# A one-byte constant in DRAM for the accumulating transfers, up to two transfers for a quad, eight term buffers, MLP evictions ahead, and a new order of an attention and token-MLP kernel

## The chip, the core and the metric

The kernel runs on one core of one Trainium2 chip. Its engines work side by side, each with an instruction queue of its own: TensorE (PE, matmuls, with its weight loads as PEld), VectorE (DVE), ScalarE (ACT), GpSimd (POOL), and SyncE (SP), which mostly issues DMAs. 16 DMA engines move data for all of them. They meet by semaphores. Matmul results stand in PSUM, which has eight banks of 512 float32 columns. The metric is device microseconds (us) of the whole program, given as the median of several runs. A profile is one further execution.

## The reference

```python
xn = layernorm(A_x)                                  # 2048 rows of 640
def A(x, wqkv, wo):                                  # attention: 32 heads of 20
    q, k, v = (x @ wqkv) split into heads
    p = softmax(q k^T * 20 ** -0.5)                  # 2048 x 2048 for each head
    return (p v, heads side by side) @ wo
def B(x, w1, b1, w2, b2):                            # MLP across the 2048 rows
    u = gelu(einsum("bsd,sf->bdf", layernorm(x), w1) + b1)      # f = 1536
    return transpose(einsum("bdf,fs->bds", u, w2) + b2)
return A_x + A(xn, wqkv, wo) * silu(B(xn, w1, b1, w2, b2))
```

Most of the work is the exponentials of the scores: 32 heads x 2048 x 2048.

## The kernel before

**Tiling.** Heads are taken in eight groups of four. A pass is one group and 512 query columns, 33 passes in all (the last 512 columns are done in two halves). A unit is one head, 128 keys and 512 queries: a score matmul (L1343) fills one PSUM bank with it. There are 2048 units. Four units of one key chunk, one for each head of the group, are a quad.

**Two ways to an exponential.** Most units go to ACT: one activation (L1373, `emit_exp`) takes two or three banks at once and writes `pt_sb`, and a matmul with V (L1459, `emit_pv`) sums it up in bank 6. The other units go to DVE by whole quads. There L1384 (`emit_op1`) turns a bank of scores into 16-bit whole numbers, which read as bf16 are a power of two made of straight pieces; four such units make one term tile `dt_sb[b]` of 4 x 512. Three more copies of the tile, raised by 32, 64 and 96, are made, and each of the four is multiplied with its own scaled V (`vs_sb`) at L1459: a quad thus costs sixteen V matmuls where four units by ACT cost four, and the mean of the four shifted lines is close to the exponential. A copy is one DVE addition (L1437, `emit_top`) into another tile. For some quads the last copy, +96, is not made by DVE: once PE has read the first tile, `emit_x` (L1408) lets POOL issue a DMA that adds a constant tile `kc_sb` (in SBUF, 16-bit, all 96) onto the first tile in place. `x_ok` says for which quads: XQ limits how far the transfers may lag, XLEFT how near the pass's end may be.

**The rest.** At the start DVE takes the statistics of the 16 row blocks (L586 to L604), POOL the powers of the variances (L600), and PE and ACT or DVE bring the transposed rows, Q, K and V into place. The MLP's matmuls (L705) and the QK and V projections of later heads run between the score matmuls in bank 7, and DVE takes them out of it (L880, L1171, L1174) or, in the start alone, ACT may (L1170, L1173). At the end the output projection (L1022) and the stores stand behind the last pass.

**What sets the order.** Nothing is scheduled on the chip: `Prog` plays the program through when it is built, with a cost for each operation, and the order that comes out is written into the engines' queues. At each step the engine that can start first takes, among its candidates, the one with the lowest priority number (`eng_cands`, `pe_cands`). A transfer is charged 950 ns of POOL, 2,900 ns of the DMA engines, and lands 5,600 ns after that (XISSUE, XMOVE, XTAIL at L48); its readers are put behind that. PLAN is a table of digits: for every 16 units claimed, `tune` sets the planner's options in OPTS by one string of it. A transfer on POOL waits for PE's reads of the tile, and the next transfer waits in POOL's queue behind it. DMAs of SP go around eight lanes, and each waits for the one before it on its lane.

Of the kernel before, what the change touches and what calls it, by code (L numbers as in the profile page):

```python
# [283 lines left out]
class _Kern:  # L284
# [9 lines left out]
    JB = 7  # L294
    RC = (1, 4, 7, 10, 13)
# [42 lines left out]
    NTILE, NLIVE, EARLY = 7, 4, True  # L338
    DLAG = 99.0
    OTA, OTD = 25.0, 0.16  # L340
    XLEFT, XQ = 20, 4000.0
    QC = ((0.5, 3.0), (3.2, 6.4), (9.0, 13.5), (14.0, 18.0), (19.0, 22.0))
# [19 lines left out]
        ("JOBF", (4, 0, 8)),  # L362
    )
    PLAN = (
        "000000000000000", "000000000000000", "000000000000000", "000000000000000", "100000000000000", "100000000000000",
        "000030000000000", "000000000000000", "000000000000000", "000030000000000", "000000000000001", "000000000000000",
        "012000000000000", "020000300000000", "002020000000000", "020000000000000", "210041000000002", "210041000000002",
        "210041000000002", "000000000000000", "000004000000000", "002020000000000", "201000000000001", "000201000000000",
        "012000000000000", "000001000000000", "000020000000000", "000030000000000", "000030000000000", "200201000000000",
        "000030000000000", "000040200000000", "000001000000000", "000000000000000", "000000000000000", "210041000000002",  # L370
        "000001000000000", "020000000000000", "010031000000002", "010000000000000", "012000000000000", "000000000010000",
        "012000000000000", "000000000000000", "120000000010000", "100000000000000", "000000000000200", "012000000000000",
        "000000000000000", "000000000000000", "000030000000000", "200000000000000", "000000000000000", "000030000000000",
        "000000000000000", "000030000000000", "000000000000000", "020000000000000", "000000000000000", "010040000000000",
        "010040000000000", "100004000000000", "000000000000000", "000104300000000", "000000000000000", "000030000000000",
        "210041000000002", "012000000000000", "000000000000000", "000001000000000", "010040000000000", "100000000000000",
        "000001000000000", "000001000000000", "000000000000000", "000050000000000", "000000000000000", "000030000000000",
        "000000000000000", "100000000000000", "000000000000000", "020000000000000", "000030000000000", "000000000000000",
        "000000000000000", "000030000000000", "000000000000000", "200041000000000", "010040000000000", "400100000000000",
        "000040000010000", "000000000000000", "000004000001000", "020000000000000", "000000000000000", "400000000000100",  # L380
        "200041000000000", "000000000000000", "000000000000000", "000004000000000", "000000300001001", "012020000000000",
        "012000000000000", "012000000000000", "000030000000000", "000000000000000", "100000000000000", "000000000000000",
        "002040000000000", "000030000000000", "000000000000000", "000030000000000", "000001000000000", "000030000000000",
        "000000000000000", "000000000000000", "010040000000000", "012000000000000", "000040000000000", "000040000000000",
        "012000000000000", "000000000000000", "000000000000000", "000040000000000", "000000000000000", "000001000000000",
        "000000000000000", "001201000000001",
# [19 lines left out]
    def build(self):  # L406
# [4 lines left out]
        with es:  # L411
# [20 lines left out]
            sb("kc_sb", [P, 4, 512], u16)  # L432
# [15 lines left out]
            t["oT_dram"] = nc.dram_tensor("oT_scratch_dram", [8 * P, S], bf)  # L448
            t["ok_dram"] = nc.dram_tensor("ok_scratch_dram", [S, 512], bf)
# [17 lines left out]
    def schedule(self):  # L467
# [719 lines left out]
        kc_sb = t["kc_sb"]  # L1187
# [216 lines left out]
        def emit_x(d):  # L1404
            b0 = d["tl"][0]
            dst = dt_sb[:, b0, :, :]
            sl_ = [S_(f"dt{b0}_{g}") for g in range(4)]
            t = pr.xdma(lambda e: e.dma_start(dst, kc_sb[:, :, :], accum_op=ALU.add), [S_("kc")] + sl_, sl_,  # L1408
                        f"dX{d['q']}_{d['c']}")
            d["tl"][3] = b0  # L1410
            d["fin"][3] = t.fin
            stats["x"] = stats.get("x", 0) + 1

        def emit_top():
# [75 lines left out]
        def emit_pv(items, quads):  # L1490
# [6 lines left out]
            for d, n_ in quads:  # L1497
                for k in range(d["pk"], d["pk"] + n_):
                    for g in range(4):
                        seq.append(("d", d, k, g))  # L1500
                    if k > (1 if self.MERGE else 0) or d["tl"][3] is not None:
                        freed.append(d["tl"][k])
# [44 lines left out]
            for d in xs:  # L1547
                emit_x(d)
# [759 lines left out]
```

## Time and profile before

| | |
|---|---|
| median of 3 runs | 745.08 us (745.07 to 745.76) |
| span of the profiled execution | 743.6 us |
| median less that span | 1.5 us |
| ACT, DVE, PE busy | 721.9, 706.5, 706.2 us |
| activations of two and of three banks | 514 and 168 |
| units by DVE | 516 (129 quads) |
| copies by DVE and by transfers | 323 and 64 |

The three runs are of the unprofiled program; the span is that of the profiled execution, from its first to its last instruction. Sums below are made against the span, and what lies around it is taken as unchanged. In the profile an engine's busy time is the union of its instructions; the mean time of one instruction is longer than the step from one to the next where two overlap. The row "A <- B: us, times, longest" of the view of waits reads: A's engine stood idle until B released it.

### The profile page before, as it was taken

Reading aid. Unit: us, or ns where it says so; the run is one execution under the profiler, and the core shown is the slowest. Engines: PE = TensorE matmul, PEld = TensorE weight load, DVE = VectorE, ACT = ScalarE, POOL = GpSimd, SP = SyncE. Lnnn points to the kernel's source line nnn. Section 1 sums busy time; section 2 is a strip of 40 time slices with the busy share of each in tenths; the row PEclk is TensorE's granted clock in tenths of the full one; section 3 lists DMA queues with packets and bytes.
Section 4 is the critical chain, followed back from the end, with each engine's and each line's share of the span. In section 5 each row is a group of like instructions: output and inputs, shape, how many; then the busy total and the mean of one; then the engine's idle time right before and its main releaser. Section 6 shows DMA issues by size and latency. Waiting matters only on the chain.

```text
span 743.6 us, 23596 instructions
## 1 busy us (share of the span) xinstructions
PE 706.2 (95%) x10472; PEld 238.1 (32%) x10486; DVE 706.5 (95%) x1295; ACT 721.9 (97%) x708; POOL 74.9 (10%) x88
## 2 busy tenths in 40 slices
PE   8899999999999989999999999999999999999997
PEld 7332222222332322323232232323333233233333
DVE  8998999999999999999999899999999999999998
ACT  5999999999999999999999999999999999999995
POOL 5300100000010000000000000011000100110000
PEclk9999999999999999999999999999999999999999
DMA  8767544432364444446234394647447993364212
GB/s 238 140 149 84 114 95 93 77 67 47 83 146 77 87 81 85 112 80 133 42 69 87 71 175 75 133 75 159 101 92 126 144 161 61 63 186 101 70 49 72
DMA packets 128955, 76.23 MB, mean 103 GB/s; under 512 B 80196, under 2 KB 119492, under 8 KB 128804
## 3 DMA queue, kind: packets, MB, share of 16 engines
q1 hardware_dynamic: 119636, 41.15, 25.3%
q0 software_dynamic: 9216, 33.56, 25.0%
q8 instruction: 82, 1.34, 0.7%
q14 instruction: 21, 0.17, 0.1%
HBM read 26.37 MB, written 10.22 MB: 49 GB/s over the span
## 4 chain that ended last, share of the span: by engine, by line
ACT 71%; PE 21%; DVE 4%; DMA 3%; issue 1%; SPq 0%; POOL 0%
ACT pt_sb L1373 69%; PE ps_all L1459 7%; PE ps_all L1343 6%; PE ps_all L705 6%; DMA dt_sb<-kc_sb 1%; DVE dt_sb L1384 1%; ACT zt_sb L906 1%; DMA bload_sb<-in_B_b_dram 1%; DVE dt_sb L1437 1%; ACT zt_sb L901 1%; PE ps_all L1022 1%; PE ps_all L690 0%; DMA regA<-in_A_x_dram 0%; SPq L1626 0%; DVE qk_sb L1174 0%
## 5 line engine op out<-in xcount | busy, mean ns | idle before, releaser
L1373 ACT ACTIVATE pt_sb<-ps_all 128x1024 bf16<-128x1024 f32 (+1 forms) x682 | 703.5, 1227 | 4.9 <-PE ps_all L1343 3.5
L1384 DVE TENSOR_SCALAR dt_sb<-ps_all 128x512 uint16<-128x512 f32 x516 | 343.0, 683 | 20.9 <-PE ps_all L1343 14.5
L1343 PE MATMUL ps_all<-qk_sb 32*128 32x512 bf16 (+1 forms) x2128 | 268.7, 376 | 22.7 <-ACT pt_sb L1373 20.1
L1437 DVE TENSOR_SCALAR dt_sb<-dt_sb 128x2048 uint16<-128x2048 uint16 x323 | 212.0, 688 | 1.6
L1343 PEld LDWEIGHTS ps_all<-qk_sb 32*128 32x128 bf16 x2128 | 67.9, 91 | 277.9 <-ACT pt_sb L1373 221.3
L1459 PE MATMUL ps_all<-dt_sb,vs_sb 128*21 128x512 bf16 (+1 forms) x1596 | 137.7, 376 | 1.3 <-DMA dt_sb<-kc_sb 0.9
L1459 PE MATMUL ps_all<-pt_sb,v_sb 128*21 128x512 bf16 (+1 forms) x1596 | 124.9, 374 | 1.3 <-DVE v_sb L1171 0.7
L1408 POOL DMA_DIRECT2D dt_sb<-kc_sb x64 | 58.4, 912 | 608.0 <-PE ps_all L1459 338.2
L705 PE MATMUL ps_all<-regC,regA 128*32 128x128 bf16 (+1 forms) x1444 | 66.5, 296 | 1.4 <-issue 1.3
L705 PE MATMUL ps_all<-regB,regA 128*32 128x128 bf16 (+1 forms) x1476 | 67.7, 297 | 0.0
L1459 PEld LDWEIGHTS ps_all<-dt_sb,vs_sb 128*21 128x21 bf16 x1596 | 35.9, 90 | 53.8 <-issue 31.2
L1459 PE MATMUL ps_all<-dt_sb,v_sb 128*21 128x512 bf16 (+1 forms) x532 | 50.7, 376 | 0.0
L705 PE MATMUL ps_all<-xnT_sb,wqk_sb 128*32 128x512 bf16 x640 | 47.7, 382 | 0.2 <-DVE qs_sb L1171 0.2
L1459 PEld LDWEIGHTS ps_all<-pt_sb,v_sb 128*21 128x21 bf16 x1596 | 29.5, 90 | 46.8 <-issue 33.4
L705 PEld LDWEIGHTS ps_all<-regB,regA 128*32 128x32 bf16 x1476 | 27.7, 96 | 24.2 <-issue 12.5
L713 PE MATMUL ps_all<-regC,regA 32*128 32x512 bf16 x92 | 35.4, 384 | 0.0
L705 PEld LDWEIGHTS ps_all<-regC,regA 128*32 128x32 bf16 x1444 | 27.1, 96 | 23.8 <-issue 12.8
L1022 PE MATMUL ps_all<-wv_sb,xnT_sb 128*128 128x128 bf16 (+1 forms) x150 | 25.6, 295 | 1.4 <-issue 1.4
L705 PE MATMUL ps_all<-wv_sb,xnT_sb 128*32 128x480 bf16 x320 | 22.8, 369 | 0.5 <-DVE v_sb L1171 0.5
L713 PE MATMUL ps_all<-regB,regA 32*128 32x512 bf16 x60 | 23.1, 385 | 0.0
L1587 DVE STREAM_TRANSPOSE tr_sb<-ps_all 128x512 f32<-128x512 f32 x31 | 22.0, 709 | 0.5 <-PE ps_all L1459 0.5
L705 PEld LDWEIGHTS ps_all<-xnT_sb,wqk_sb 128*32 128x32 bf16 x640 | 13.6, 95 | 19.2 <-issue 8.8
(88 smaller groups left out, 360.5 us busy)
## 6 DMA issues: line engine op xcount, KB each, us to landing
dt_sb<-kc_sb POOLq DMA_DIRECT2D x64, 512.0 KB, 5.5
regA<-in_B_w_dram SPq DMA_DIRECT2D x6, 1024.0 KB
regA<-in_B_w_dram SPq DMA_DIRECT2D x8, 768.0 KB
qk_sb<-qk_scratch_dram SPq DMA_DIRECT2D x56, 80.0 KB
qk_scratch_dram<-qs_sb SPq DMA_DIRECT2D x32, 128.0 KB
regA<-in_A_x_dram SPq DMA_DIRECT2D x6, 640.0 KB
ok_scratch_dram<-on_sb SPq DMA_DIRECT2D x96, 20.0 KB
out_dram<-regC SPq DMA_DIRECT2D x3, 640.0 KB
```

Of the source, the lines that this page charges most:

```text
L705: fns.append(lambda e, c=c, e_=e_: e.matmul(oc(c, e_), lhsT[:, c:e_], rhs, start=start, stop=stop, tile_position=(0, c)))
L713: row = lambda g: (lambda e: e.matmul(oc(0, 128), lhsT[32 * g:32 * g + 32, :], rhs[32 * g:32 * g + 32, :], start=False, stop=False, tile_p ...
L901: steps.append(("act", lambda e: e.activation(tt_, tt_, AF.Tanh, scale=1.5957691216), [stt], [stt], f"th{j}", ac(n)))
L906: steps.append(("act", lambda e: e.activation(tt_, z, AF.Tanh), sz, [stt], f"th2_{j}", ac(n)))
L1022: steps.append(("pe", lambda e, c=c: e.matmul(ap, oT_sb[:, c, b * 128:(b + 1) * 128], wo_ap[:, c, c0:c0 + n], start=(opens and c == 0), st ...
L1343: t = pr.pe(lambda e, outp=outp, lhsT=lhsT, rhs=rhs, g=g: e.matmul(outp, lhsT, rhs, start=True, stop=True, tile_position=(32 * g, 0)), rea ...
L1373: tk = pr.act(lambda e: e.activation(outp, inp, AF.Exp, scale=math.log(2.0) / 128.0), reads=[bank_slot[b] for b in banks[:n]], writes=[S_( ...
L1384: tk = pr.dve(lambda e: e.tensor_scalar(w, src, WOFF, 0.0, ALU.add, ALU.max), reads=[bank_slot[bk]], writes=[S_(f"dt{d['tl'][0]}_{g}")], n ...
L1408: t = pr.xdma(lambda e: e.dma_start(dst, kc_sb[:, :, :], accum_op=ALU.add), [S_("kc")] + sl_, sl_, f"dX{d['q']}_{d['c']}")
L1437: tk = pr.dve(lambda e: e.tensor_scalar(dst, src, dk, None, ALU.add), reads=[S_(f"dt{b}_{g}") for b in inb for g in range(4)], writes=[S_( ...
L1459: pr.pe(lambda e: e.matmul(outp, lhsT, rhs, start=(k == 0), stop=last, tile_position=(0, 32 * g)), reads=reads, writes=[bank_slot[AB]], na ...
L1587: steps.append(("dve", lambda e: e.transpose(tr_sb[:, :], ps(AB)), [bank_slot[AB]], [S_("tr")], f"epT{q}", 632.0))
```

## The change

Six edits. The constant for the accumulating transfers is no longer a 16-bit tile in SBUF: POOL fills two rows of 64 16-bit words with the bytes 96 and 64 (`kc_sb`, 256 bytes for each partition instead of 4,096), and two DMAs of SP spread them into a DRAM tensor `kc_dram` of bytes; a transfer reads 2,048 bytes for each partition there and widens them to 16 bits while it adds. The 8th term tile takes the place of the old constant (NTILE 7 to 8). A quad may give two copies to transfers: DVE then makes only the +32 copy, and when PE has read the first tile, +64 is added to it in place, and when PE has read the +32 tile, +64 is added to that (96 in all); `x2_ok` decides with XLEFT2 and XQ2. DVE's MLP work that holds a bank gets the priority number EVJ (36 or less, by the plan 19 or 45) where it had 45 (`eng_cands`). Six more options stand in the plan, and its table is another one.

```diff
-    NTILE, NLIVE, EARLY = 7, 4, True
+    NTILE, NLIVE, EARLY = 8, 4, True
+    EVJ = 36.0
+    XLEFT2, XQ2 = 40, 1000.0
...
+        ("EVJ", (36.0, 19.0, 45.0)),
+        ("XLEFT", (20, 14, 28, 99)),
+        ("XLEFT2", (40, 32, 26, 99)),
+        ("XQ2", (1000.0, 3000.0)),
+        ("NLIVE", (4, 5, 6)),
+        ("D_GUARD", (8, 16, 24)),
...
-        "000030000000000", "000000000000000", "000000000000000", "000030000000000", "000000000000001", "000000000000000",
+        "000000000000000000000", "000000000000000000001", "000000000000000003000", "000000000000000000000", "000000000000000000000", "010031000000002000000",
...
-            sb("kc_sb", [P, 4, 512], u16)
+            sb("kc_sb", [P, 2, 64], u16)
+            t["kc_dram"] = nc.dram_tensor("kc_scratch_dram", [2 * P, 2048], dt.uint8)
...
+        def x2_ok(d):
+            if "kc" not in done or pr.xpipe > pr.T["dve"] + self.XQ2:
+                return False
+            return d["q"] > a_cur[0] or a_left(d["q"]) >= self.XLEFT2
+
-        def emit_x(d):
-            b0 = d["tl"][0]
+        def emit_x(d, k0, k1):
+            b0 = d["tl"][k0]
+            i = 0 if k1 - k0 == 3 else 1
             dst = dt_sb[:, b0, :, :]
+            src = kc_dram[i * P:(i + 1) * P, :].rearrange("p (g n) -> p g n", g=4)
             sl_ = [S_(f"dt{b0}_{g}") for g in range(4)]
-            t = pr.xdma(lambda e: e.dma_start(dst, kc_sb[:, :, :], accum_op=ALU.add), [S_("kc")] + sl_, sl_,
-                        f"dX{d['q']}_{d['c']}")
+            t = pr.xdma(lambda e: e.dma_start(dst, src, accum_op=ALU.add), [S_(f"kc{i}")] + sl_, sl_,
+                        f"dX{d['q']}_{d['c']}_{k1}")
...
+        def feed_x(d):
+            if d["x"] == 1 and d["pk"] >= 1 and d["tl"][3] is None:
+                emit_x(d, 0, 3)
+            if d["x"] == 2 and d["pk"] >= 1 and d["tl"][2] is None:
+                emit_x(d, 0, 2)
+            if d["x"] == 2 and d["pk"] >= 2 and d["tl"][3] is None:
+                emit_x(d, 1, 3)
...
-            if k == 2 and not self.MERGE and x_ok(d):
-                d["x"] = True
+            if k == 1 and not self.MERGE and x2_ok(d):
+                d["x"] = 2
                 dtop.pop(0)
-                if d["pk"] >= 1:
-                    emit_x(d)
+                feed_x(d)
+            elif k == 2 and not self.MERGE and x_ok(d):
+                d["x"] = 1
+                dtop.pop(0)
+                feed_x(d)
...
-        add_job("kc", [("pool", lambda e: e.memset(kc_sb[:, :, :], int(self.DK[3])), [], [S_("kc")], "kc", 1800.0), ("tag", "kc")],
-                (), 43.0)
+        kcl = []
+        for i in (0, 1):
+            kcs = bass.AP(kc_sb, 64 * i, [[128, P], [0, 16], [1, 64]]).bitcast(dt.uint8)
+            kcd = kc_dram[i * P:(i + 1) * P, :].rearrange("p (r n) -> p r n", r=16)
+            kcl.append(("pool", lambda e, i=i: e.memset(kc_sb[:, i, :], int(self.DK[3 - i]) * 257), [], [S_(f"kcs{i}")], f"kcs{i}", 150.0))
+            kcl.append(("dma", lambda e, kcd=kcd, kcs=kcs: e.dma_start(kcd, kcs), [S_(f"kcs{i}")], [S_(f"kc{i}")], f"kc{i}", 262144))
+        add_job("kc", kcl + [("tag", "kc")], ("qk0_0_3",), 41.0)
...
-                    c.append((j.prio, pr.ready(eng, s[2], s[3]), lambda j=j: do_step(j, eng)))
+                    p_ = min(j.prio, self.EVJ) if eng == "dve" and j.bk is not None and not ramp[0] else j.prio
+                    c.append((p_, pr.ready(eng, s[2], s[3]), lambda j=j: do_step(j, eng)))
```

In the built program this gives, of activations, 516 of two banks and 164 of three (514 and 168 before), so 1,524 units by ACT where there were 1,532; on DVE 524 units at L1384 (516), 317 copies (323); on POOL 76 transfers (64); on PE 24 more V matmuls that read term tiles and 8 fewer that read `pt_sb`. By the planner's own count 24 quads give two copies to transfers and 28 give one (0 and 64 before).

The first place is ACT's queue in the start of the program, from its first exponential on (`pt_sb`); `qk_sb` and `v_sb` are taken out of PSUM there. Before:

```order
L1373 ACTIVATE pt_sb<-ps_all 128x1536
L1173 ACTIVATE qk_sb<-ps_all 128x256
L1170 ACTIVATE qk_sb<-ps_all 128x256
L1373 ACTIVATE pt_sb<-ps_all 128x1536 x4
L1170 ACTIVATE qk_sb<-ps_all 128x256
L1373 ACTIVATE pt_sb<-ps_all 128x1536
L1170 ACTIVATE qk_sb<-ps_all 128x256
L1373 ACTIVATE pt_sb<-ps_all 128x1536 x11
L1373 ACTIVATE pt_sb<-ps_all 128x1024 x4
```

And with the change:

```order
L1382 ACTIVATE pt_sb<-ps_all 128x1536 x2
L1179 ACTIVATE v_sb<-ps_all 128x2x8x20
L1382 ACTIVATE pt_sb<-ps_all 128x1536 x2
L1179 ACTIVATE qk_sb<-ps_all 128x256
L1382 ACTIVATE pt_sb<-ps_all 128x1536
L1179 ACTIVATE qk_sb<-ps_all 128x256
L1382 ACTIVATE pt_sb<-ps_all 128x1536 x9
L1179 ACTIVATE qk_sb<-ps_all 128x256
L1179 ACTIVATE v_sb<-ps_all 128x8x20
L1382 ACTIVATE pt_sb<-ps_all 128x1536 x2
L1382 ACTIVATE pt_sb<-ps_all 128x1024 x5
```

Three evictions have come over from DVE: one of V (320 columns) into the first run of four exponentials, and one of Q or K (256) and one of V (160) two activations before the end of the run of eleven.

The second place is POOL's queue, from the fill of the ones in `v_sb` on. Before:

```order
L568 MEMSET v_sb 128x512x2
L1643 MEMSET kc_sb 128x2048
L600 TENSOR_TENSOR st_sb<-st_sb,cst_sb 128x2 x6
L622 TENSOR_TENSOR st_sb<-st_sb,cst_sb 128x8
L1835 MEMSET idb_sb 128x128
L1408 DMA dt_sb<-kc_sb 128x2048 x44
L1757 MEMSET wqk_sb 128x640
L1408 DMA dt_sb<-kc_sb 128x2048 x20
```

And with the change:

```order
L577 MEMSET v_sb 128x512x2
L609 TENSOR_TENSOR st_sb<-st_sb,cst_sb 128x2 x6
L631 TENSOR_TENSOR st_sb<-st_sb,cst_sb 128x8
L1868 MEMSET idb_sb 128x128
L1675 MEMSET kc_sb 128x64 x2
L1424 DMA dt_sb<-kc_scratch_dram 128x2048 x52
L1790 MEMSET wqk_sb 128x640
L1424 DMA dt_sb<-kc_scratch_dram 128x2048 x24
```

The fill of the constant no longer stands ahead of the first powers of the variances; two short fills stand behind all of them, and twelve more transfers follow.

The third place is PE's queue where it first waits for transfers (`sem_x0` to `sem_x3` tell of them); `dt_sb,vs_sb` are V matmuls of a copy, `qk_sb` are score matmuls. Before:

```order
L705 MATMUL ps_all<-xnT_sb,wqk_sb 32x512 x19
L1459 MATMUL ps_all<-dt_sb,vs_sb 21x512 [waits sem_x0]
L1459 MATMUL ps_all<-dt_sb,vs_sb 21x512 x3
L1343 MATMUL ps_all<-qk_sb 128x512 [waits sem_act]
L1343 MATMUL ps_all<-qk_sb 128x512 x2
```

And with the change:

```order
L1352 MATMUL ps_all<-qk_sb 128x512 [waits sem_dve]
L1487 MATMUL ps_all<-dt_sb,vs_sb 21x512 [waits sem_x0]
L1487 MATMUL ps_all<-dt_sb,vs_sb 21x512 x3
L1487 MATMUL ps_all<-dt_sb,vs_sb 21x512 [waits sem_x1]
L1487 MATMUL ps_all<-dt_sb,vs_sb 21x512 x3
L1352 MATMUL ps_all<-qk_sb 128x512 [waits sem_act]
```

Where PE waited for one transfer and then went on to scores, it now takes the copies of two transfers in a row.

More of the change, by code (lines that the diff above doesn't have):

```diff
@@ L367 @@
[L367 to L371, printed above, removed]
@@ L1186, in schedule @@
         tfree = list(range(self.NTILE))
-        kc_sb = t["kc_sb"]
+        kc_sb, kc_dram = t["kc_sb"], t["kc_dram"]
         dlive = [0]
@@ L1500, in emit_pv @@
                         seq.append(("d", d, k, g))
[L1501 removed]
+                    if k > (1 if self.MERGE or d["x"] == 2 else 0) or (d["tl"][3] is not None and not d["x"]):
                         freed.append(d["tl"][k])
                 d["pk"] += n_
[L1504 removed]
+                if d["x"]:
                     xs.append(d)
@@ L1903, in pe_cands @@
                 k = 0
-                while k < len(quads) - 1 and quads[k][1]["x"] and quads[k][1]["pk"] == 3:
+                while k < len(quads) - 1 and quads[k][1]["x"] and quads[k][1]["pk"] >= 4 - quads[k][1]["x"]:
                     k += 1
@@ L2045, in dve_load @@
             for d, k in dtop:
-                x += (1730.0 if k == 1 else 1130.0) if self.MERGE else 600.0 * ((3 if x_ok(d) else 4) - k)
+                x += (1730.0 if k == 1 else 1130.0) if self.MERGE else 600.0 * ((2 if k == 1 and x2_ok(d) else 3 if x_ok(d) else 4) - k)
             return x
@@ L2211, in loads @@
                 d += (1730.0 if x["fin"][1] == 0.0 else 1130.0 if x["fin"][3] == 0.0 else 0.0) if self.MERGE else (
-                    597.0 * sum(f == 0.0 for f in x["fin"][1:3 if x["x"] else 4]))
+                    597.0 * sum(f == 0.0 for f in x["fin"][1:4 - (x["x"] or 0)]))
             return a - done_cost["act"], pe - done_cost["pe"], d - done_cost["dve"]
```

45 lines of the change are left out of this document (25 added, 20 removed).

## The prediction

> **What bounds the kernel now.** First the page's busy times, its chain of waits, and the program cut into three stretches (columns: length, then busy time and instructions of PE, weight loads, DVE, ACT, POOL, then clock, DMA share, GB/s).
>
> ```profile
> span 743.6 us, 23596 instructions
> PE 706.2 (95%) x10472; PEld 238.1 (32%) x10486; DVE 706.5 (95%) x1295; ACT 721.9 (97%) x708; POOL 74.9 (10%) x88
> ...
> ACT 71%; PE 21%; DVE 4%; DMA 3%; issue 1%; SPq 0%; POOL 0%
> ```
>
> ```profile
> 0.00:26.00 26.00, 21.69 (x248) 15.96 (x248) 22.63 (x80) 16.65 (x21) 12.80 (x20) 1.00 0.88 201
> 26.00:730.00 704.00, 674.66 (x10085) 216.89 (x10098) 673.37 (x1195) 700.46 (x684) 62.09 (x69) 1.00 0.50 99
> 730.00:744.00 14.00, 9.81 (x140) 5.26 (x140) 10.46 (x23) 4.81 (x5) 0.00 (x0) 1.00 0.27 95
> ```
>
> Between 26 and 730 us ACT is idle 704.0 - 700.5 = 3.5 us, PE 29.3 and DVE 30.6. So ACT sets the length of the middle, and a change there is worth what it takes off ACT as long as PE and DVE keep feeding it. They have 4% to spare each, in pieces; PE's 21% of the chain says that it often releases ACT at the last moment. The start (ACT idle 9.4 us of 26) and the end (9.2 of 14) are set by other things. The clock is 1.00 throughout.
>
> **The exponentials.** The groups by shape price a unit (count, then busy time, mean ns of one, idle before):
>
> ```profile
> L1373 ACT ACTIVATE pt_sb<-ps_all 128x1024 bf16<-128x1024 f32 x514 | 498.0, 1124 | 1.9 <-PE ps_all L1343 1.0 <-PE ps_all L713 0.2
> L1384 DVE TENSOR_SCALAR dt_sb<-ps_all 128x512 uint16<-128x512 f32 x516 | 343.0, 683 | 20.9 <-PE ps_all L1343 14.5 <-PE ps_all L713 4.2
> L1373 ACT ACTIVATE pt_sb<-ps_all 128x1536 bf16<-128x1536 f32 x168 | 250.5, 1543 | 3.0 <-PE ps_all L1343 2.4 <-PE ps_all L1459 0.3
> L1437 DVE TENSOR_SCALAR dt_sb<-dt_sb 128x2048 uint16<-128x2048 uint16 x323 | 212.0, 688 | 1.6
> ```
>
> ```profile
> L1373 ACT ACTIVATE pt_sb<-ps_all 128x1024 bf16<-128x1024 f32 (+1 forms) x682 | 703.5, 1227 | 4.9 <-PE ps_all L1343 3.5
> ```
>
> A third bank adds 1543 - 1124 = 419 ns. The 682 activations hold 514 x 2 + 168 x 3 = 1,532 units, 641.9 us at that price; the other 61.6 us of 703.5 are 90 ns for each activation. The change leaves 516 and 164: eight units and two activations fewer, 3.35 + 0.18 = **-3.5 us**. Bounds: -3.35 (units alone) and -4.5 (8 x 1124 / 2). Two quads more go to DVE instead.
>
> **Evictions moved onto ACT.** Three in the start: 320, 256 and 160 columns.
>
> ```profile
> 12.37 1.44 ACT L1373 ACTIVATE pt_sb<-ps_all 128x1536 bf16<-128x1536 f32 x1
> ...
> 15.29 5.48 ACT L1373 ACTIVATE pt_sb<-ps_all 128x1536 bf16<-128x1536 f32 x4 [0.92 <-PE ps_all L1343]
> 20.63 0.42 ACT L1170 ACTIVATE qk_sb<-ps_all 128x256 bf16<-128x256 f32 x1
> 21.53 1.45 ACT L1373 ACTIVATE pt_sb<-ps_all 128x1536 bf16<-128x1536 f32 x1 [0.48 <-PE ps_all L1343]
> 22.88 0.38 ACT L1170 ACTIVATE qk_sb<-ps_all 128x256 bf16<-128x256 f32 x1
> 23.14 4.14 ACT L1373 ACTIVATE pt_sb<-ps_all 128x1536 bf16<-128x1536 f32 x3
> ```
>
> The one at 22.88 holds the next exponential back 0.26 us for 256 columns; 736 columns make 0.75 us if ACT has no gap for them, and nothing where they fall into gaps like those of 0.92 and 0.48. I take **+0.6**, since two of the three now stand in a run without gaps.
>
> **The fill of the constant leaves the start.** Rows of POOL, DVE and PE in order of time (start, length):
>
> ```profile
> 2.76 2.86 POOL L568 MEMSET v_sb<- 128x1024 bf16 x1
> 5.36 1.96 POOL L1643 MEMSET kc_sb<- 128x2048 uint16 x1
> 7.43 1.59 POOL L600 TENSOR_TENSOR st_sb<-st_sb,cst_sb 128x2 f32<-128x2 f32 x2
> ```
>
> ```profile
> 5.79 1.56 DVE L597 TENSOR_SCALAR st_sb<-st_sb 128x2 f32<-128x2 f32 x1
> 5.84 1.50 DVE L586 BATCH_NORM_STATS2 bst_sb<-regA 128x6 f32<-128x320 bf16 x1
> ...
> 7.65 0.17 DVE L597 TENSOR_SCALAR st_sb<-st_sb 128x2 f32<-128x2 f32 x1
> 8.18 0.80 DVE L604 TENSOR_SCALAR regC<-regA,st_sb 128x640 bf16<-128x640 bf16 x2 [0.36 <-POOL st_sb L600]
> ```
>
> ```profile
> 8.69 0.81 PE L656 MATMUL ps_all<-idb_sb,regC 128*128 128x128 bf16 x10 [1.29 <-DVE regC L604]
> ```
>
> ```profile
> 7.34 0.54 ACT L785 ACTIVATE wp_sb<-wqk_sb 128x400 bf16<-128x400 bf16 x1 [0.70 <-DMA wqk_sb<-in_A_wqkv_dram]
> ```
>
> The first power at 7.43 stands in POOL's queue behind the fill, which ends at 7.32. What it reads, L597, takes 0.17 us the second time but 1.56 the first, ending with the fill too. Without the fill POOL is free at 5.62 and L597 done at about 5.96, so the power, DVE's row scaling, and the transposes for which PE waits 1.29 us come up to 7.43 - 6.05 = 1.4 us sooner. What is late next: the second weight copy ends at 7.88, before the Q and K matmuls would need it; the later row blocks come by DMA, and the first stretch's DMA share of 0.88 leaves those little room. So between 0 and -1.4; I take **-1.0**, nearer the full step because ACT runs almost without a gap from 23 us on and keeps what it has gained by then.
>
> **PE.** 24 more V matmuls on term tiles (32 of two quads, less 8 of eight units). Two pieces of the chain:
>
> ```profile
> 497.52 0.54 PE ps_all L1459 x8
> ...
> 498.38 0.76 PE ps_all L1459 x12
> ```
>
> Four more cost 0.22 us, so 24 cost 1.3 us. They lie in PE's 29 us of idle time, but by its 21% of the chain I charge **+0.3** (bounds 0 and 1.3).
>
> **DVE.** Eight more L1384 at 343.0 / 516 = 0.66 us and six fewer L1437 at 212.0 / 323 = 0.66: +1.3 us, hidden in 30 us of idle time, 0 (+1.3 if that cover is gone).
>
> **The transfers.**
>
> ```profile
> q0 software_dynamic: 9216, 33.56, 25.0%
> ```
>
> ```profile
> L1408 POOL DMA_DIRECT2D dt_sb<-kc_sb x64: 872/872/1510, 51.2 to 700.9; - x64
> ...
>   PEld ps_all L1459: 1.2, 1
>   PE ps_all L1459: 0.9, 1
> ...
> DMA to landing us min/median/max: 4.5/5.5/11.1
> ```
>
> ```profile
> 0.00:10.00 10.00, 7.51 (x70) 6.82 (x70) 6.71 (x22) 3.09 (x5) 8.08 (x14) 1.00 0.79 232
> ```
>
> A transfer takes 0.25 x 743.6 / 64 = 2.9 us of all 16 DMA engines. The plain loads of the first 10 us run at 232 / 0.79 = 294 GB/s, by which 512 KB take 1.8 us. With half the source bytes it should cost 1.8 to 2.9, unless widening bytes is slower; no row shows that. POOL's 12 more issues at 0.87 us fit its 642 us of idle time in the middle. The price is the landing. The planner keeps readers 0.95 + 2.9 + 5.6 = 9.45 us behind the issue, more behind a queue of transfers; the median landing is 5.5, and of 64 only one made PE wait, 1.2 us. So +4 us would be hidden in the median case: I take 0.
>
> The source now lies in DRAM. [...]
>
> **The stores of the constant, EVJ, the new order.** The two DMAs stand on SP behind the small bias loads and ahead of the first Q/K stores, and the first transfers wait for them. SP waits a few rows ahead for work of DVE anyway,
>
> ```profile
> SPq L1601 <- DVE on_sb L1595: 12.8, 1, 12.8
> ```
>
> and DVE makes the copies until then, which the 317 contain. EVJ adds no instruction: an MLP eviction goes ahead of a copy (38), which frees bank 7 earlier and the copy's reader later, both hidden by PE's other candidates. What the new order does to ACT's waits I set to 0, with bounds of 3.5 us either way: it can save no more than the 3.5 us of idle time, and I let it lose as much.
>
> **Sum.** -3.5 + 0.6 - 1.0 + 0.3 = -3.6 us: a span of 740.0. The median lies 745.08 - 743.6 = 1.5 above the span, so **741.5 us**; and, since the terms' bounds will hardly all fall on one side, the root of the squares of half their widths (0.6, 0.4, 0.7, 0.6, and half of the order's 3.5) gives some 2.1 either way, 739.4 to 743.6.
>
> **The rivals.** *PE and DVE carry what ACT sheds.* All three engines are busy for 95% or more, so work given to DVE and PE may come back as waits of ACT: -3.5 + 0.75 (evictions in full) + 0 (loads hold the start) + 1.3 + 1.3 = -0.2, 744.9 us. For it: the chain's pieces where PE follows PE. Against: 29 and 31 us idle. 0.17.
>
> *Transfers land late.* Slower than before. Place: PE at the V matmuls of a pair's copies, with the scores for ACT queued behind them, and DVE's next quads wanting the tiles. Two or more transfers now go out together, and MLP weight loads share the engines. Price: the 1.2 us that the one late landing cost. Three more such waits take back the 3.6 us, five make the kernel slower by over 0.2%; seven of 76 give 741.5 + 8.4 = 749.9. Against it: up to 4 us of cover at the median. [...] 0.13.
>
> *The order wins as well.* ACT's 3.5 us of waits vanish too: 738.0. Against: the order before was no looser than 0.5%. 0.07.
>
> That bytes are no cheaper to transfer changes nothing in the sum, since it rests on fewer units for ACT.
>
> **How the numbers follow.** The forecast has 0.63. The range from 738.8 to 746.5 holds it, the first rival whole and the mild half of the second; about 0.16 is left out. About 0.2%, 1.5 us, is what a measurement of this kernel tells from none: faster takes the forecast but for 0.01 at its upper edge, and the third rival, 0.69; same takes that edge and the first rival, 0.18; slower the second, 0.13.
>
> **What would show it.** Right: exponentials' busy time down by about 3.5 us; ACT idle in the middle near 3.5; the first power near 6.1 us and the first exponential (12.37 now) near 11.3; waits of PE on transfers under 3 us in all; PE and DVE less idle by a little over 1 us. Wrong: a first exponential still near 12.4; ACT's waits on scores above 7 us; PE's waits on transfers of several us, or transfers that take over 4 us of the DMA engines; ACT's idle time at either end longer.

## The result

The changed kernel takes 757.0 us (median; 754.95 to 758.18) against 745.08 before: a ratio of 1.0159, 95% interval [1.0142, 1.0176]. It is slower, by 11.9 us, where 741.5 was forecast. The profiled execution has a span of 753.2 us, the shortest of the changed kernel's; its differences below are therefore a little smaller than those of the medians.

Busy times, transfers, chain and exponentials of the page after:

```profile
span 753.2 us, 23668 instructions
...
PE 716.3 (95%) x10512; PEld 239.2 (32%) x10512; DVE 706.4 (94%) x1294; ACT 719.6 (96%) x709; POOL 87.1 (12%) x101
...
q0 software_dynamic: 10944, 39.85, 27.4%
...
ACT 69%; PE 20%; DMA 7%; DVE 2%; issue 1%; SPq 0%; DVEq 0%
...
L1382 ACT ACTIVATE pt_sb<-ps_all 128x1024 bf16<-128x1024 f32 (+1 forms) x680 | 700.1, 1230 | 15.8 <-PE ps_all L1352 11.0
```

ACT has less to do, as meant (exponentials 703.5 to 700.1 us), but the idle time ahead of its exponentials has grown from 4.9 to 15.8 us, and the chain's share of DMA from 3% to 7%. The program cut into stretches (length; then busy time and instructions of PE, weight loads, DVE, ACT, POOL; clock; DMA share; GB/s) says where:

```profile
0.00:26.00 26.00, 22.28 (x254) 16.44 (x254) 22.34 (x82) 17.28 (x22) 11.24 (x19) 1.00 0.87 205
...
85.00:92.00 7.00, 4.71 (x45) 0.89 (x45) 4.43 (x8) 2.35 (x3) 0.00 (x0) 0.76 0.35 107
92.00:306.00 214.00, 210.46 (x3131) 63.93 (x3130) 209.50 (x360) 213.84 (x213) 22.38 (x23) 1.00 0.45 87
306.00:314.00 8.00, 5.57 (x93) 1.54 (x79) 4.32 (x8) 4.39 (x5) 0.00 (x0) 0.79 0.83 202
314.00:450.00 136.00, 130.91 (x2065) 41.42 (x2059) 130.50 (x226) 135.67 (x133) 16.66 (x18) 1.00 0.55 106
450.00:457.00 7.00, 5.19 (x60) 1.27 (x60) 2.91 (x5) 4.02 (x5) 0.00 (x0) 0.76 0.50 123
```

Three stretches of 22 us together hold 11.2 us of ACT's idle time (7.0 - 2.35, 8.0 - 4.39, 7.0 - 4.02), while in the 350 us between them it idles 0.5. In these three, and nowhere else in the middle, TensorE's clock is not 1.00: 0.76 over 7 us is 7 x 0.24 x 2 = 3.4 us at half clock, and 8 x 0.21 x 2 is the same; slices of 0.4 us inside them show 0.50. Over the whole span: ACT's busy time -2.3, its idle time in the start -0.6, between 26 and 730 us +11.2 (3.5 to 14.7), at the end +1.3, which makes +9.6 us, the difference of the two spans.

The first stall in order of time, for SP, POOL, DVE, PE and ACT (start, length, engine, line, count, idle time before and its releaser):

```profile
71.99 3.51 SPq L1629 DMA_DIRECT2D ok_scratch_dram<-on_sb  x4
75.60 5.47 SPq L744 DMA_DIRECT2D qk_scratch_dram<-qs_sb  x1
86.47 1.41 SPq L783 DMA_DIRECT2D qk_sb<-qk_scratch_dram  x4
```

```profile
71.47 4.18 POOL L1424 DMA_DIRECT2D dt_sb<-kc_scratch_dram  x4 [38.21 <-PE ps_all L1487]
```

```profile
86.54 0.69 DVE L1183 TENSOR_SCALAR qs_sb<-ps_all 128x512 bf16<-128x512 f32 x1 [4.79 <-DMA qk_scratch_dram<-qs_sb]
```

```profile
87.29 1.13 PE L714 MATMUL ps_all<-xnT_sb,wqk_sb 128*32 128x512 bf16 x12 [4.31 <-DVE qs_sb L1183]
```

```profile
89.00 1.02 ACT L1382 ACTIVATE pt_sb<-ps_all 128x1024 bf16<-128x1024 f32 x1 [4.71 <-PE ps_all L1352]
90.51 1.02 ACT L1382 ACTIVATE pt_sb<-ps_all 128x1024 bf16<-128x1024 f32 x1 [0.48 <-PE ps_all L1352]
```

Read it upwards. ACT waits for scores, PE for bank 7, DVE (which is to empty the bank into `qs_sb`) for the 128 KB store of the block that stood in `qs_sb` before. SP came to the store at 75.60, and it had landed when DVE went on, at 86.5: 10.9 us. Half of that is SP's own issue, whose row is 5.47 us long. In the kernel before, where two transfers stand here and the first is issued at 76.28, after the store, a store of the same kind was issued in 0.43 us, and SP, which waits for it ahead of the loads of `qk_sb`, went on 3.5 us after its start:

```profile
75.16 0.43 SPq L735 DMA_DIRECT2D qk_scratch_dram<-qs_sb  x1
78.70 2.04 SPq L774 DMA_DIRECT2D qk_sb<-qk_scratch_dram  x4
```

From 71.5 us on the changed kernel has four accumulating transfers, two doubled quads, back to back; at 27.4% x 753.2 / 76 = 2.72 us each they hold the 16 DMA engines for 10.9 us in all. The other two places look alike on PE:

```profile
309.20 0.55 PE L714 MATMUL ps_all<-regC,regA 128*32 128x128 bf16 x23 [2.43 <-issue]
```

```profile
451.81 1.30 PE L714 MATMUL ps_all<-regB,regA 128*32 128x512 bf16 x20 [2.04 <-DMA regA<-in_B_w_dram]
```

Three transfers were issued from 298.2 us, four from 434.7. In the second case what came late were MLP weights that SP issued from 436.20 on, and again the issue itself is long, 9.42 us for two loads:

```profile
434.66 3.57 POOL L1424 DMA_DIRECT2D dt_sb<-kc_scratch_dram  x4 [18.15 <-PE ps_all L1487]
```

```profile
436.20 9.42 SPq L856 DMA_DIRECT2D regA<-in_B_w_dram  x2
```

In the first case the trace shows no releaser. The transfers' own readers, whose landing the prediction priced, hardly waited (a wait of the weight load, PEld, and of the matmul behind it can be the same time, so the two rows are not added):

```profile
who waited for it (us, times):
  PEld ps_all L1487: 0.5, 1
  PE ps_all L1487: 0.2, 1
...
DMA to landing us min/median/max: 4.8/7.7/14.2
```

### The profile page after: what moved, and what is told of

Same layout as the page of the kernel before. It is cut to its first block, busy times and chain, and to the rows that moved or that the text cites. A ratio compares the mean times of both kernels' runs of the same rounds, so it can differ in the third digit from the quotient of the medians.

```text
span 753.2 us, 23668 instructions
## 1 busy us (share of the span) xinstructions
PE 716.3 (95%) x10512; PEld 239.2 (32%) x10512; DVE 706.4 (94%) x1294; ACT 719.6 (96%) x709; POOL 87.1 (12%) x101
## 3 DMA queue, kind: packets, MB, share of 16 engines
q0 software_dynamic: 10944, 39.85, 27.4%
## 4 chain that ended last, share of the span: by engine, by line
ACT 69%; PE 20%; DMA 7%; DVE 2%; issue 1%; SPq 0%; DVEq 0%
ACT pt_sb L1382 68%; PE ps_all L1487 7%; PE ps_all L1352 6%; PE ps_all L714 5%; DMA regA<-in_B_w_dram 2%; DMA qk_scratch_dram<-qs_sb 1%; DMA dt_sb<-kc_scratch_dram 1%; PE ps_all L1031 1%; DMA xnT_sb<-oT_scratch_dram 1%; ACT zt_sb L915 1%; DMA regA<-in_A_x_dram 1%; ACT zt_sb L910 1%; DMA xnT_sb<-regC 0%; DVE dt_sb L1393 0%; DVE bst_sb L595 0%
## 5 line engine op out<-in xcount | busy, mean ns | idle before, releaser
L1382 ACT ACTIVATE pt_sb<-ps_all 128x1024 bf16<-128x1024 f32 (+1 forms) x680 | 700.1, 1230 | 15.8 <-PE ps_all L1352 11.0
L1393 DVE TENSOR_SCALAR dt_sb<-ps_all 128x512 uint16<-128x512 f32 x524 | 347.3, 681 | 24.9 <-PE ps_all L1352 13.3
L1461 DVE TENSOR_SCALAR dt_sb<-dt_sb 128x2048 uint16<-128x2048 uint16 x317 | 208.0, 686 | 1.4
L1487 PE MATMUL ps_all<-dt_sb,vs_sb 128*21 128x512 bf16 (+1 forms) x1620 | 140.9, 380 | 1.5 <-DVE dt_sb L1461 1.2
L1424 POOL DMA_DIRECT2D dt_sb<-kc_scratch_dram x76 | 72.5, 1115 | 603.6 <-PE ps_all L1487 478.2
L1487 PE MATMUL ps_all<-pt_sb,v_sb 128*21 128x512 bf16 (+1 forms) x1588 | 123.1, 374 | 1.7 <-DVE v_sb L1180 0.8
L714 PE MATMUL ps_all<-regB,regA 128*32 128x128 bf16 (+1 forms) x1480 | 69.7, 300 | 2.8 <-DMA regA<-in_B_w_dram 2.0
L722 PE MATMUL ps_all<-regC,regA 32*128 32x512 bf16 x88 | 33.8, 385 | 0.0
L1031 PE MATMUL ps_all<-wv_sb,xnT_sb 128*128 128x512 bf16 (+1 forms) x160 | 28.7, 301 | 0.5 <-DMA xnT_sb<-oT_scratch_dram 0.5
L714 PEld LDWEIGHTS ps_all<-xnT_sb,wqk_sb 128*32 128x32 bf16 x640 | 12.9, 95 | 23.5 <-issue 11.5
```

Of the source, the lines that this page charges most:

```text
L714: fns.append(lambda e, c=c, e_=e_: e.matmul(oc(c, e_), lhsT[:, c:e_], rhs, start=start, stop=stop, tile_position=(0, c)))
L722: row = lambda g: (lambda e: e.matmul(oc(0, 128), lhsT[32 * g:32 * g + 32, :], rhs[32 * g:32 * g + 32, :], start=False, stop=False, tile_p ...
L1031: steps.append(("pe", lambda e, c=c: e.matmul(ap, oT_sb[:, c, b * 128:(b + 1) * 128], wo_ap[:, c, c0:c0 + n], start=(opens and c == 0), st ...
L1382: tk = pr.act(lambda e: e.activation(outp, inp, AF.Exp, scale=math.log(2.0) / 128.0), reads=[bank_slot[b] for b in banks[:n]], writes=[S_( ...
L1393: tk = pr.dve(lambda e: e.tensor_scalar(w, src, WOFF, 0.0, ALU.add, ALU.max), reads=[bank_slot[bk]], writes=[S_(f"dt{d['tl'][0]}_{g}")], n ...
L1424: t = pr.xdma(lambda e: e.dma_start(dst, src, accum_op=ALU.add), [S_(f"kc{i}")] + sl_, sl_, f"dX{d['q']}_{d['c']}_{k1}")
```

## The experiments

Two readings to begin with. Theory 1: the transfers crowd out other DMA traffic. Theory 2: the transfers are innocent, and the new order, EVJ and the evictions moved onto ACT lose the time. Four kernels had the change's order of every engine and differed in the transfers and their constant alone. The code here and below is shortened; where a line of it says in words what changes, it is a description.

**Quarter transfers**

```diff
-            dst = dt_sb[:, b0, :, :]
-            src = kc_dram[i * P:(i + 1) * P, :].rearrange("p (g n) -> p g n", g=4)
+            dst = dt_sb[:, b0, 0, :]
+            src = kc_dram[i * P:(i + 1) * P, 0:512]
```

> The changed kernel, order and instructions untouched, but each of the 76 accumulating transfers adds the constant to the first 512 of a partition's 2,048 elements only; three quarters of the additions are left out, and the powers that they would make are wrong. Theory 1 (the transfers crowd other DMA traffic out: while up to four of them run back to back, the stores at 86 us, the weight loads at 450 us and an instruction fetch at 307 us wait): a transfer takes under 1.2 us of the DMA engines instead of 2.72, ScalarE's idle time between 26 and 730 us falls from 14.7 us to 3 to 6, TensorE's granted clock never drops to 0.5, and the time is 740 to 745 us. Theory 2 (the new order, the eviction cost of 36 and the evictions moved onto ScalarE lose the time, the transfers are innocent): the stalls stay and the time is 753 to 758 us.

Measured: 740.56 us (740.09 to 741.26), 0.9942 of before [0.9927, 0.9957]. Its middle:

```profile
26.00:730.00 704.00, 684.07 (x10196) 219.55 (x10200) 678.53 (x1203) 701.57 (x689) 75.94 (x82) 1.00 0.34 67
```

ACT idles 2.4 us there, less than before the change, and the clock is 1.00. A transfer holds the engines 8.8% x 739.5 / 76 = 0.86 us. Theory 2 is out: order, EVJ, evictions and units give about the forecast time as soon as the transfers are short. The whole loss, 16.4 us against this kernel, hangs on their length.

**Shorter rows: 1,024 and 512 bytes.** The same bytes, in rows a quarter or an eighth as long (k = 4 and 8): the transfers' queue shows 528 and 1,040 packets for each transfer where it showed 144. Theory 1a is that the length of a row is what holds the others up; the author's estimate by it was 741 to 748 us for rows of 1,024 bytes and 740 to 747 for rows of 512.

```diff
+            dst = dt_sb[:, b0, :, :].rearrange("p g n -> p (g n)").rearrange("p (a n) -> p a n", a=k)
+            src = bass.AP(kc_dram, i * P * 2048, [[2048, P], [0, k], [1, 2048 // k]])
```

> The changed kernel, order and instructions untouched, everything still computed; each partition's 4,096 bytes go as four packets of 1,024 bytes instead of one of 4,096, because the constant is read four times from the same 512 bytes. [...] Theory 1b (what counts is how long the DMA engines are busy in all, not how it is cut): the stalls stay, 753 to 758 us. Theory 2 (the order is at fault): 753 to 758 us.

> As the kernel with packets of 1,024 bytes, with eight packets of 512 bytes per partition; everything is still computed. [...] Theories 1b and 2: 753 to 758 us.

Measured: 756.45 us, 1.0155 [1.014, 1.017], and 771.7 us, 1.0339 [1.029, 1.0388]. With rows of 1,024 bytes, the transfers' queue, the first stall on ACT, and who waited for the transfers:

```profile
q0 software_dynamic: 40128, 39.85, 32.8%
```

```profile
87.50 1.02 ACT L1382 ACTIVATE pt_sb<-ps_all 128x1024 bf16<-128x1024 f32 x1 [3.02 <-PE ps_all L1352]
```

```profile
who waited for it (us, times):
  PEld ps_all L1487: 4.9, 6
  PE ps_all L1487: 2.8, 5
```

Theory 1a fell as the cause of the lost time. A row does take less than a third of the time (with the rows taken as spread evenly over the 16 engines, 3.26 us for 32 rows on an engine are 102 ns, 2.72 us for eight are 340), but there are four times as many, so a transfer takes 32.8% x 755.0 / 76 = 3.26 us, and 3.94 us with 512 bytes. The stall by the late weights shrank as 1a would have it (2.10 to 0.48 us); the one behind the store fell only from 4.71 to 3.02, since the store still landed after 9.3 us; the one at 310 us grew from 2.84 to 3.32; and the readers of the transfers now waited, PEld 4.9 us and PE 2.8. Shorter rows give a little and take it back by longer transfers.

**A constant of two bytes**

> The changed kernel, order and instructions untouched, everything computed; the constant in DRAM has two bytes per element instead of one, so the source of a transfer is 512 KB instead of 256 KB. If a packet's time goes by the bytes read from DRAM, a transfer takes 3.5 us or more of the DMA engines instead of 2.72 and the time rises to 760 us or more; if it goes by the bytes or elements that are written, a transfer takes 2.7 to 2.9 us and the time stays at 754 to 759 us. Theory 2 expects no change, 754 to 758 us.

Measured: 762.74 us, 1.0239 [1.021, 1.0269], against 757.0 with one byte; a transfer takes 29.4% x 763.5 / 76 = 2.95 us. Neither sentence held: twice the source bytes lengthen a transfer by 0.24 us only, not by 0.8, but the program is 5.7 us longer. In the profiled execution (765.29 us, the longest of the four) ACT's wait at the first place is 6.16 us, where it was 4.71, and a fourth one, of 4.31 us, stands at 660 us. So the one byte per element is worth having in this order: with rows of 4,096 bytes, 0.24 us more for a transfer went with 5.7 us more for the program.

What was open now was whether all transfers harm (theory T) or only the places where they pile up (theory R).

**Quarter transfers at the three places only**

```diff
+            if f"dX{d['q']}_{d['c']}_{k1}" in (the four from 71.5 us, three from 298.2, four from 434.7):
+                dst, src = dt_sb[:, b0, 0, :], kc_dram[i * P:(i + 1) * P, 0:512]
```

> The changed kernel, order untouched; only the eleven transfers of the three places where they pile up (four issued at 71.5 to 73.3 us, three at 298.2 to 301.2, four at 434.7 to 436.4) add the constant to a quarter of their elements, the other 65 are whole; three quarters of the additions of the eleven are left out. Theory R (runs: the loss comes from the few places where three or four transfers stand back to back for 8 to 11 us just as a store, a weight load or an instruction fetch is due): ScalarE's gaps of 4.7, 2.8 and 2.1 us and the three stretches of half clock go, 743 to 747 us. Theory T (total: the loss grows with all the time that the transfers hold the DMA engines): 11 of 76 transfers bring 11/76 of the 16.4 us that the quarter transfers brought, 754 to 756 us.

Measured: 742.53 us (742.24 to 743.4), 0.9967 [0.9954, 0.998]. With 65 of 76 transfers whole, 14.5 of the 16.4 us are back. SP's issue of the store takes 0.43 us again (5.47 in the changed kernel), that of the two weight loads 1.96 (9.42). Theory T, which said 754 to 756, is out; theory R gave 743 to 747, a little too much.

**The kernel before with quarter transfers**

```diff
-e.dma_start(dst, kc_sb[:, :, :], accum_op=ALU.add)
+e.dma_start(dst[:, 0, :], kc_sb[:, 0, :], accum_op=ALU.add)
```

> The kernel before, order untouched, with each of its 64 transfers cut to a quarter of its elements; three quarters of the additions are left out. Theory R: before has hardly any pile-up, so little is to be had, 742.5 to 745 us. Theory T: its 64 transfers hold the DMA engines 2.9 us each, 186 us against the 206 of the change, so a quarter of them brings nearly as much as it did there, 728 to 733 us.

Measured: 743.08 us, 0.9973 [0.9962, 0.9984]. Before, 64 whole transfers of 2.9 us cost 744.74 - 743.08 = 1.7 us in all, where theory T wanted 12 and more. With short transfers on both sides the changed kernel is 743.08 - 740.56 = 2.5 us ahead: this is about what units, start and order are worth together.

**The kernel before with a one-byte constant in DRAM**

```diff
-memset(kc_sb[P, 4, 512], 96)  at GpSimd's start, 1.96 us
+memset(kc_sb[P, 64], 96 * 257) and a store of it to DRAM, 16 times over, at about 35 us
```

> The kernel before, order of all engines untouched but for GpSimd: the long memset of the constant leaves its place before the first power, and a short memset and a store of one-byte constants to DRAM stand at about 35 us instead; the transfers read that. Everything is computed. If the one-byte DRAM source is harmless by itself: the start gains up to 0.9 us, a transfer takes 2.6 to 2.8 us of the DMA engines instead of 2.9, 743 to 745 us. If reading the constant from DRAM is what slows other traffic: 747 us or more.

Measured: 745.48 us (744.17 to 748.19), 1.0007 [0.9996, 1.0019]: no difference, so the source in DRAM costs nothing by itself, in an order that loses little to its transfers (1.7 us). (A pile-up with the source in SBUF was not run; the kernels with short or spaced transfers keep the source in DRAM and lose the stalls.) But the start gained nothing either, which the expectation had as possible up to 0.9 us. The first power does come at 5.86 us instead of 7.43; then, with the old order, DVE sits on a row block's load:

```profile
8.85 0.49 DVE L609 BATCH_NORM_STATS2 bst_sb<-regA 128x6 f32<-128x320 bf16 x1 [1.14 <-DMA regA<-in_A_x_dram]
...
9.61 0.61 DVE L689 COPY xnT_sb<-ps_all 128x512 bf16<-128x512 bf16 x2
```

and the copies (L689) that Q and K wait for stand behind that. The first exponential starts at 12.33, against 12.37 before.

**Transfers 4.5 us apart.** Nothing is left out here: a transfer that stands less than 4.5 us behind the one ahead of it waits for a later exponential as well, as far as its first reader leaves 9 us behind the issue.

```diff
+            at = min(max(x.t0, last + gap), max(x.t0, rd - 9000.0))
+            if at > x.t0 + 300.0:
+                x.waits["act"] = (the last exponential that the plan has done by `at`)
```

> The changed kernel, everything computed, each engine's order untouched; transfers that stood back to back wait in addition for a later exponential, so that they start 3 to 4.5 us apart where their readers leave room for it (the four at 71.5 to 73.3 us start over 9.5 us instead of 2). Theory R: the pile-ups are broken, most of the 16 us comes back, 741 to 748 us, faster than before if nothing else is lost. Theory T: the same total, 754 to 758 us. If the room of the readers was needed: TensorE waits on landings for several us and the time is 750 us or more with those waits in the trace.

Measured: 742.98 us (742.07 to 746.99), 0.9982 [0.9966, 0.9997]. The same 76 whole transfers, only at other moments, and 14 of the 16.4 us are gone.

**Who is crowded out**

```diff
+ stores of one pass at 72 us: 512 rows of 160 bytes instead of 2,048 of 40
+ weight loads at 436 us: dst[:, 0:1, :] of 12
```

> The changed kernel with its transfers whole and its order untouched, but the other traffic of two of the three places thinned: the four stores of one pass's results at 72 to 75 us write 512 packets of 160 bytes of unprocessed values instead of 2,048 of 40, and the two weight loads at 436 us bring one twelfth of their bytes; those results and that part of the MLP are not computed. If it is what lies on the same queue that the transfers hold up (the stores at 72 us keep the store of the query and key block behind them from landing; the 1.5 MB of weights come late): ScalarE's gaps at 89 and 454 us fall under 1 us each, the one at 311 us, which had no such traffic, stays at 2 to 3.5 us, and the time is 746 to 750 us. If the store of the block is slow by itself beside the transfers, whatever is ahead of it: the gap at 89 us stays above 3 us, 751 to 754 us. If the pile-up costs in another way (TensorE, the port of SBUF): all three gaps stay, 754 to 758 us.

Measured: 752.05 us (751.2 to 754.94), 1.0099 [1.0075, 1.0122]. The second of the three readings: the stall at 450 us is gone (ACT runs from 443.66 on without a gap), the one at 311 us stays, and the one at 89 us stays too.

```profile
72.35 3.24 SPq L1634 DMA_DIRECT2D ok_scratch_dram<-on_sb  x4
75.69 1.12 SPq L744 DMA_DIRECT2D qk_scratch_dram<-qs_sb  x1
85.82 1.43 SPq L783 DMA_DIRECT2D qk_sb<-qk_scratch_dram  x4
```

```profile
88.70 1.02 ACT L1384 ACTIVATE pt_sb<-ps_all 128x1024 bf16<-128x1024 f32 x1 [4.05 <-PE ps_all L1354]
...
311.79 1.02 ACT L1384 ACTIVATE pt_sb<-ps_all 128x1024 bf16<-128x1024 f32 x1 [3.00 <-PE ps_all L1354]
```

The store, issued at 75.69, holds SP until 85.82: 10.1 us instead of 10.9 with a quarter of the rows ahead of it (the same bytes). SP's issue of it is short now, 1.12 us instead of 5.47, and still it lands no sooner to speak of. It is not the many small rows ahead that make it late; what is left beside it are the transfers.

**How far apart, and which**

> As the kernel with transfers 4.5 us apart, now 6 us apart where their readers leave 9 us behind the issue; everything is computed. Theory R: no pile-up is left but those that the readers force; 741.5 to 743.5 us, and fewer of the executions at 746 us that the spacing of 4.5 had. If the readers' room is used up: waits of TensorE on transfers of 3 us and more, 744 to 748 us.

> The changed kernel, everything computed; only the eleven transfers of the three pile-ups are set 4.5 us apart, the other 65 start as in the change. Theory R: these three places are nearly all of the loss, 742.5 to 746 us. If spacing helped because all transfers were thinned out: 748 to 755 us.

> The kernel before, everything computed, with the same rule of 4.5 us between its transfers (26 of 64 start later, by 0.3 to 4.8 us). Its quarter transfers brought 1.7 us, so spacing brings at most that: 743.3 to 745 us. That bounds what the changed kernel with spacing owes to the spacing alone: if the new order is worth its 2 to 3 us, the changed kernel with spacing stays 1 to 2 us ahead of this one.

With 6 us: 745.07 us (742.03 to 750.76), 1.0002 [0.9981, 1.0024]. This expectation was wrong. In the profiled execution (747.79 us, one of the longer ones) the block's store, beside two transfers still, holds SP for 5.9 us; at 91 us DVE waits 2.08 us for the next store and PE 0.81 us for a transfer to land, and ACT loses 1.9 us at 93 us. But the last two transfers of the first place were issued at 81.0 us, as at 80.3 with 4.5 us between, where ACT had no such gap, so this trace doesn't explain the 2 us between the medians. More spacing does not simply bring more; why not stays open.

With 4.5 us at the three places alone: **742.72 us** (742.02 to 744.83), 0.9967 [0.9956, 0.9979]. This one computes everything and is faster than both kernels. Its transfers, its store and its exponentials at the first place, and its middle:

```profile
73.27 1.05 POOL L1446 DMA_DIRECT2D dt_sb<-kc_scratch_dram  x1 [38.21 <-PE ps_all L1509]
77.11 0.88 POOL L1446 DMA_DIRECT2D dt_sb<-kc_scratch_dram  x1 [2.78 <-PE ps_all L736]
81.64 2.31 POOL L1446 DMA_DIRECT2D dt_sb<-kc_scratch_dram  x2 [3.65 <-PE ps_all L1374]
```

```profile
77.38 0.44 SPq L766 DMA_DIRECT2D qk_scratch_dram<-qs_sb  x1
81.16 1.47 SPq L805 DMA_DIRECT2D qk_sb<-qk_scratch_dram  x4
```

```profile
69.56 26.56 ACT L1404 ACTIVATE pt_sb<-ps_all 128x1024 bf16<-128x1024 f32 x26
```

```profile
26.00:730.00 704.00, 683.24 (x10181) 219.36 (x10178) 677.08 (x1200) 701.34 (x689) 76.56 (x82) 1.00 0.54 109
```

The store lets SP go on after 3.8 us, ACT runs 26 exponentials without a gap, and idles 2.7 us in the whole middle.

The same spacing in the kernel before: 745.25 us, 1.0007 [0.9993, 1.0022], no difference, though 743.3 to 745 had been given. What makes the spaced kernel faster than before is therefore the change's own order and units, once the pile-ups are out of the way.

## Why the prediction was wrong

**The step that failed** is "The transfers": "The price is the landing ... So +4 us would be hidden in the median case: I take 0." It asked only who waits for the transfers, and there it was right: their readers waited 0.5 us (PEld) and 0.2 us (PE), once each. It did not ask who else needs the DMA engines while two doubled quads' transfers stand back to back. A block's store (10.9 us instead of 3.5 before and 3.8 when spaced) and weights (SP's issue of two loads 9.42 us instead of 1.96 with short transfers) came late, and PE stood still for 2.43 us at 307 us; behind each of these ACT ran dry, and PE fell to half clock for 3.4 us. The term taken as 0 measures 757.0 - 740.56 = 16.4 us, of which 14.5 lie at three places. The sum gave the term no bounds either; only the order's 3.5 us each way, of which half went into the range, left room for a loss (with all of the 3.5 the root would be 3.7 us, not 2.1, and still far from 16). The working had the number from which to see it: 2.9 us of all 16 DMA engines for a transfer, times four. The change's planner cannot see it, since it adds up the transfers (`xpipe`) and all other DMAs (`pipe`) as two pipes that never slow each other.

**"Transfers land late"**, the rival with a chance of 0.13, had the sign, but its place (PE at the V matmuls of a pair's copies) and its price (1.2 us for each late landing, 749.9 us) were those of the readers. The landing did rise, from 5.5 to 7.7 us in the median, within the planner's 9.45 us behind the issue; the longest took 14.2. It named the MLP's weight loads as sharing the engines with the transfers; here the loads were what came late.

**The source in DRAM** alone did no harm in the kernel before (1.0007).

**The exponentials**, -3.5: measured -3.4 (703.5 to 700.1).

**The fill leaves the start**, -1.0: the first power came at 6.02 (6.1 forecast), the first exponential at 11.44 (11.3 forecast), 0.9 us earlier. The reason was half of it: in the old order the same step moved the first power but not the first exponential. The new order of DVE and ACT in the start is needed too. And the gain was not kept as forecast: ACT's idle time in the first 26 us is 0.6 us shorter here, and 0.2 us longer than before in the profiled execution of the quarter kernel (9.57 against 9.35).

**Evictions, PE, DVE and order**, +0.6, +0.3, 0 and 0, were not measured one by one. Together with the two terms above they stand in the quarter kernel: 740.56 us where the sum gave 741.5, so together they were no worse than taken. That the two are so close is in part luck: in the quarter kernel's profiled execution (span 739.5) ACT's busy time is 3.9 us lower than before, its idle time 0.2 higher in the start, 1.1 lower in the middle and 0.7 higher at the end, which makes -4.1, where the sum had -3.6 from -3.5 of exponentials and -1.0 of the start. "PE and DVE carry what ACT sheds" (744.9) is out: with the same units on PE and DVE, ACT's waits in the middle fell to 2.4 us.

**What was to show it wrong** did: ACT's waits on scores stand at 11.0 us, above the 7 named, and ACT's idle time at the end is 1.3 us longer. The longer end goes with the new order and not with the pile-ups: from 730 us on ACT idles 8.8 us before and 8.9 before with quarter transfers, 10.1 in the changed kernel, and still 9.5 with its quarter transfers and 10.0 with the three places spaced.

**Open:** why PE stood still for 2.43 us at 307 us. It goes when the three transfers there are cut or spaced. The trace names no releaser. That PE's own instructions came late by DMA fits what it shows: the queue that the page calls "instruction" moved nothing between 294.0 and 306.8 us and then one packet at 306.90, when PE had just stopped; PE went on at 309.20. That packet came 14.4 us behind the one ahead of it. In the same order with the eleven transfers short the same two packets are 12.0 us apart, with the eleven spaced 11.5, and PE does not stop; with rows of 1,024 bytes they are 14.5 apart, and PE stops for 2.63 us. Whose instructions a packet holds the trace doesn't tell, and no run delayed one alone, so this is likely and not shown. Nor is such a stop the changed kernel's alone: the profiled execution of the spaced kernel before (750.51 us) has one of 2.28 us at 578 us.

## What to carry to other kernels

A DMA that hardly anybody waits for is not free (here 76 whole ones took 16.4 us more than quarter ones, and their readers waited 0.5): price the time that it holds the DMA engines against whatever else is due on them just then, and look at the longest run of such transfers back to back, not at their mean share (27% here). Before adding transfers, list the stores and loads with a deadline in the same microseconds; moving the transfers of three places by a few microseconds was worth 14 us. And cut a suspected cost to a quarter with the order untouched: that one run told transfers from order at once.

## What the runs showed of the hardware that was not expected

- **The time of an accumulating transfer went with its bytes, and the number of its rows added a little.** 512 KB take 2.72 us of the 16 engines in rows of 4,096 bytes, 3.26 in rows of 1,024 and 3.94 in rows of 512; 128 KB in rows of 1,024 take 0.86, about a quarter. With the rows taken as spread evenly over the engines, from 8 to 32 rows on an engine a further row adds (3.26 - 2.72) / 24 = 23 ns, from 32 to 64 (3.94 - 3.26) / 32 = 21 ns.
- **One byte or two in the source** makes 2.72 against 2.95 us from DRAM in the changed kernel. In the order before it is 2.90 with two bytes from SBUF and 24.5% x 746.3 / 64 = 2.86, the store of the constant included, with one byte from DRAM. So half the source bytes save 1% to 8%.
- **What a second queue gets beside such transfers.** The 128 KB store landed after 10.9 us beside transfers in rows of 4,096 bytes, 9.3 in rows of 1,024 and 8.2 in rows of 512. With rows of 1,024 bytes ACT's stall behind the weight loads fell from 2.10 to 0.48 us; the store gained 1.6 us of 10.9. How the DMA engines divide their time between the queues is not settled by these runs.
- **Half clock behind stops of PE.** In the changed kernel PE stood still for 4.31, 2.43 and 2.04 us, and each time the clock was at 0.50 for 3.4 us afterwards. The kernel before with the constant in DRAM shows the same behind a stop of 1.75 us at 578 us.
